# Block-sparse attention and a gated convolution FFN: a new written-out order, with six more dummy products on TensorE in the head

## The chip, the cores and the metric

The kernel runs on one core of a Trainium2 chip. Its engines work side by side, each through its own queue in order: TensorE (PE in the profile, with its weight loads as PEld), VectorE (DVE), ScalarE (ACT), GpSimd (POOL) and SyncE (SP). GpSimd, SyncE and ScalarE also issue DMA transfers. The metric is the device time of one execution, in microseconds (us). The median of the three runs shown here is the time that a kernel is judged by; one further execution was profiled.

## The reference

The inputs are q, k and v of shape 4 batches x 8 heads x 768 tokens x 64, in float32, and an integer table of sampled blocks. In short:

```python
scores = q @ k.T / 8                        # per batch and head, 768 x 768
mask   = |blk_i - blk_j| <= 1, first and last block rows and columns, 3 sampled blocks per row
attn   = softmax(where(mask, scores, -1e9))
x      = (attn @ v) as [4, 768, 512]        # heads side by side
h      = relu(x @ w_in)                     # 512 -> 1024
c      = conv_w[0]*h[s-1] + conv_w[1]*h[s] + conv_w[2]*h[s+1]   # along the tokens, per channel
out    = (h * sigmoid(c)) @ w_out           # 1024 -> 512, float32
```

## The kernel before, in words

**Attention.** All scores are computed, also masked ones: the mask is in 24 more rows (one per block of 32 tokens) that are appended to the 64 rows of q and k, so that one product over 88 rows gives score plus mask. The scores come out transposed (keys on the partitions). Two heads make a pair P, with 16 pairs in all; a query half of 384 tokens of one batch is a segment (the last one is cut in two, so there are 9). The scores of a segment are cut into units of 8 blocks of 128 x 128, and there are 144 units. A unit u is: two score operations `s` (number 2u and 2u+1, 512 columns of products each, line 761) into one of two PSUM tiles `st`; one `exp` on ScalarE over 128 x 1024 (line 773) into one of six tiles `pt`; two `av` operations of four 65-column products each (line 798). Score tiles alternate, so scores of unit u+2 wait until the exp of unit u has read its tile.

**FFN.** When a segment's four pairs are through, VectorE divides by the row sums (`rcp`, `norm`, line 709), the result is transposed (`x_tr` on TensorE with an eviction `x_cp`, or `x_xb` by a transposing DMA from SyncE), and TensorE multiplies with w_in (`f1`, line 895). The result goes through `relu` (ScalarE, line 915, or VectorE, line 917), the convolution is `mul` and `add` on VectorE (lines 947 and 955), then `tanh` on ScalarE (994), `g1` and `g2` on VectorE (997, 1002), the product with w_out (`f2`, line 830), an eviction `ev` (ScalarE or VectorE) and the store `out` from SyncE.

**PSUM.** Two score tiles of two banks, two banks `av`, two banks `mix`. The banks `mix` are shared by the transposes of q, k and x, by f1 and by f2, so each such operation waits for the eviction two users before it.

**Head.** Pair 0 is loaded in float32 over SyncE and ScalarE (`ld_k0`, `ld_q0`), cast (`cast_k`, `cast_q`), transposed (`k_tr`, `q_tr`, lines 460 and 500) and copied (`k_cp`, `q_cp`) beside the mask rows (`m_k`, `m_q`). All later pairs come over GpSimd's queue with a cast in the DMA (line 239). Before and between these, TensorE runs dummy products on a zeroed tile (line 230): 13 of 256 columns (`warm`) and NFILL of 128 columns (`fill`).

**Order.** Every operation is put into a graph by `op(name, ...)`, with the engines that may do it. Nothing schedules at run time: `put_down` reads the string `ORDER`, in which two letters name an operation by its place in the graph, one more letter names the engine where there is a choice, and one more the buffer where one is taken. So ORDER alone sets each engine's sequence, the split of evictions between ScalarE and VectorE, and which buffer each operation gets. In this document an operation is named by its name and its number in the graph, counted from 0 within the name (relu 2 is the third relu).

Of the kernel before, what the change touches and what calls it, by code (L numbers as in the profile page):

```python
# [21 lines left out]
0k0l1B00m0n0o0p1N11O1I01Z01/21AA202b1171CV1DV11G1vA0XV520535715810V5401G012V1HV1b0q0r0s0t0u0v0w0x0y5c00z5911P1
0A5d0K1S02d32e1V12725h11MA0135e25i5501QV11UV1TV1RV565a5b1J05m05n5j32r04M2p2140B5f0C5v15w5o45g5k5x51LV1KV1+V10L
1e11f5A05B2102415C05F15G0D0E5K05L5l5p5H15M25q15y22V225V26V23V5T15U5V35r02cV25z5D5s155Y05Z5E2f15+4611625I5J2i0
6352gV3660676802hV2kV2jV5N5O5W06b16c5X1W15/6d16k06l60646p16m26q65695P15Q6r3161i1XV2qV36a6e6g26h1h6u06v6f16n6o
6z16A6s6t6w46i06I06J1YV1j1k1d5t16x6y6B56N16C6O5uV06jV6K06D6P15R16S06T6U26L06M6E26F5SV6G00+6HV6X16Q1o6Y2s4N2l34O
2D04P1p1m2F14Q1c1n2G4R1q4S2EV42R16Z31lih1ii70071ie0ifigV0ijA7917a724ik1il2807e07f7b5iC0iEiD29V2aViFimA7g06R7j1
7k7l1in16VioipV6W7o07p2t06+iG7x17y6/iw173ix7q27z34T1r4U2T24ViK1iL2uV47502vViM767C07DiyA7417c7d7H17E47I2w17h7i
2m02xV2oV2yV7m7M07n7r7s7A07B7J52nV7N7t1iN77178V12SV07F7R17Siq0iriH7O07T17uiIisViJ0iO7+07/7G7K7L831848028537v1
2H07P7wV2IV07Q8807UiP7W22JViQ7V1898d181827X8a42U4W1s8e86it1iuivV4X1t4Y2+2iR8f58m08n7Y0878b7ZV8r18s8o08c2K18g8t1  # L30
iS2iT2MV8w08x8hiz08y28B18C8i02LV8jiAiBViV8p0iU8G08H8q8u8v8k18D3i+3j0iWi/8I48O18P8Q5j608T08U8V0322iX8z8A8E8F8J
8Y18K18R8S8Z2W02V12X8lV2ZVj12YV8+1910j792932j2jc1jd9919a8W8X8/90j39e09f944Z3034+31iYiZ2/V1959b3j8je9g59j19kj4
8L1j50/331349628M8N2jfjgV09l136V39j9jaA19o09p9q4jl13a03c9t1jmji0jnA35V9u971gjjjkV9B03e04/370509Cjr1js9c09d9v0
2z0512N1jG0jHjI3b3i9G19H2A09hjJ2CV2BVjK9D29L09i9MjtA9I39m9N5jo1jpjqV9Q1jx09Rjy9n9r9sjLjzA9S19Y09wju1jvjwA9Z3l
3m13o38V29x19EjO1jMjPjQjR9y0jW29+4a119F9Ja2jX9zjA0a60a7a30a823j13n3u3x3y2jSjT9K9O9P2O12PVjN2QVjZjYab19Tac9U9/0
jBjCV9V1983fjU9Wag0j+jb3q13d33p4ad3jD1aha0ai5jEjFAao1apa4a59Ak23ks0a9k3jV9Xk4k5k6aq1j/aaaeafat0auajak1ay1arav4
kg1asazkhaA0aD0awktaEaxk7aL1aMaBaCk0k1aF2kiku3raN3aQ0aRk8k9aGkjaS1aHkvkkA2al2am3hV3AaV1aWa+0a/3v2kwA3aX5b00aI0
aJ3gV3sV3C0ky1kz3kV3kAV1kB0kCkDVkW0kXkZaO0b31aPb4b52kN1aTbb0kH0aU3z3G3H03J3K33M3L3R3S1kIkOkJAkPAbcbg1bhbd4kY3tV
k+kE0kFkGVl21l3l4l5l6aYaZb1b2b6bl0kK1b71bebmbi3bfbq1kLbrkMVb81an0km0knbjla2lck/bn1by0lb3wV43B0ldbzl0b9kokpbs5l7
bA0kqA1bD1kT1bEkUbI0bJkQ0bF2kVAbK4l8leaKkxkl3N1kRkSVli3lkl11lfbN1l9ljlgllbkbobpbtbubv2lmka1bObP3bS0bT3Dlhbw3EV  # L40
3FVbU1kbkckdbB0keA3b+1b/c05bCbGbHlw0bLc30c4lxc81lnbMbQc9lq1lrc50ba3Ololpbxcd0ce3U3V03Z3Wkf3XjhlybRlzbVbW1ca2cf4
3PV13QVlAV2c1cl1cmcq0c2lscrcn3lC0lDcv13IV03TV1bX0bYcwcs1ltcx5lEVlF0lGlBlHVl+0l/m0m1m2cA0cBc6c7cblI0cF1cccGluA3
cC046471lJcgchlL1co0cH2lMcN0cpctcOlKAlNVci1m61m7cjcucS1cTm3cylO0lR1cP3cU13+0bZ1cX0cYczlPcDcElScZ5lQAm8m9cIcJ1m4
mamb3Y43lTVme2mgmfcK2mccLmhm5d01d1d80cQcRcVcWc+d9lU0lVd24da0dd1lWVdec/lX1df24b4849ck4c13/di0djd3lYdn1domdmidk3
d4cMdb04k4l2lZAdcmA0ds0dtmu14424adgdp1mm3momnmpd50mqdhd6du4mjmkml4pdA1dBmBdld7dC0mr40V242msdF0dGdmdqmvdrdvdw1
dK1dLdDdEdH2mCmwdIdP0dQdM3dR1mtmDmEV0lvdX1dYdx1dymxdJdNdOdSe00dTdZ44m4h4dmyA24ykre1e51e20e6e75mS0mV1mWd+0mTdz2
41VdU2dVea0ebef1mUV0mXAne0nfngnhni4q0dW4z3d/ege34n4i04D4Am/1e4ec3mY0en0eon0n1V4oeh1e8es1ete9edmZ4eV3m+V4fVnm1nn
45V2ep4njnknpnoeeeiek0elnqnl0mF4E1mzex0eymG1mHmImJez0eu5n20eC0mKA3eDej1eqereK1n3eE3em4rn4AeLeM4nrevn51n6eP0eweA
n7VeQeBeFeGeN0nb0eU1eVnu2eH1eInweR5eW0n81ncn9naAeZ0e+f21eOf3e/3nvnxmM1mNeSeTeXeYfa0f44ndVnsny4jV3nznC3fbf0f1nt
f5ff1f61fgfc5fh0mOeJmPnDnEfdfk0o00flnFfefp1o1mQA1o31fqo4nGnH4sV4nAnB4tVo2Afm3nInJo5AnQ0nR4B4v4w14CmRmL4Ffx0fy  # L50
4xV4oq0osfr2nSnK1fz4fC1fDnTfH04J4K2fIfE14LV0orotounUV0fJ5ovnLnMnNfM1fNnOA2f724GV0f84HVfifR0fjnW0nXnZ1n+fnfO0nYA
n/AfS4ufofsftfZ1f+o90owoxfA0oaoi1okfT3ojfu0olfvomg20fBg3fFo61o7f/2g44obAg71fGfKfLg8fPfQo8Voy2fUozfW1onnVf904g4I
fwof0gc0g91oBoooAopgdge5oc1odoeAgk1ogohAglfV1g0g1g5gp0gm0oU1gqg6gaoVgu1gbgvgfggoO0oPoCoG3oHoJoIfXoKgr3oDgw2gn0
gD0gogsgtgEgI1gJoLgh2oEoFgigF4fYgK1oWgxoQgN0gOoMoNoXoYV1gP5gygW1oRgXp41p5p6g/0p7gjoSA3h0gY0gz0p8A0pa0pbpd1peh41
pcV1pfVpy0gAh13pAh5hd0pj0pg1pkphgG1h62nPoZplApiAhegHgLhi1gMgQgRhf4pzpBgB0gCA1gZ0g+hjpp1pG1pCpHpIpJpKhn0hk1pDpq
pm0pnpoAprAgS1gThohw1pO2pPpEpRhxhy5h2h3h7h8ps0pto+1o/hg1p0hhpuAp1h92pQpLhp0pMpF1pShahB1gU0hChlhmhqhrp2A2gVAhs0
hthD3pv1pwhb0hz0hK0pxAhcVpThLhM2pNhu0hvVhAhT1hUqh1hEqipW3pYqn0hY0hG1qoqjApXpZp+hV4hF1hNhOq21p/hZi51i6qpApUhHpV
q0hP2q3hW0hI0q4q1h+1q5hJV2hXqe0qfhQqy0qAqzi70qBh/i01i8i9q6A1qk1qgAi10i2i30qlqO1qq2ia1qrqPibi4AqmAp9p3qtqsqG3q80
q9hR1hSAqaic1idAqbqcA0rf1rgrhAr60r7quqvqCqIqRqwq7qdoTqxr8AqDrx0rc1rdryreAri1rjr90raqEqFrz2rk0r01rAqHrBqJrlrmqK
qQrs0rtr1rbArn1ru2qW0rorp0rqrrqLqXrC0rI1rO2rJrPrvqSrwqMqTqUqNrDrQrKrRrLrMA2rSArNqVr2rTr3r4V1r5qYqZq+A0q/rErF  # L60
# [989 lines left out]
```

## Time and profile before

| what | value |
|---|---|
| median of three runs | 207.91 us (207.61 to 208.0) |
| the profiled execution's own time | 207.34 us |
| its span, first to last instruction | 205.5 us |
| TensorE busy | 198.0 us (96%) |
| VectorE busy | 185.2 us (90%) |
| ScalarE busy | 190.7 us (93%) |
| GpSimd busy | 60.8 us (30%) |
| moved by DMA | 25.20 MB |
| exp of one unit (line 773) | 144 of 1044 ns on average |

The span lies 1.84 us below the execution's own time; those 1.84 us lie around the instructions. The busy time of an engine can overlap itself, since its instructions are pipelined: an exp that the profile shows with 1.02 to 1.08 us is followed by the next 0.90 to 0.92 us after its start. Waits are read from the idle time before an instruction and from what is named behind the arrow as its releaser. In the chain of waits, a piece belongs to the engine that was waited for.

### The profile page before, as it was taken

The numbers are of one execution on the slowest core, as the hardware profiler recorded it, in microseconds if no ns is written. First come the engines' busy times: TensorE is split into PE (matmuls) and PEld (weight loads), VectorE is DVE, ScalarE is ACT, GpSimd is POOL, SyncE is SP. The second block draws the span as 40 slices with busy tenths as digits, with TensorE's granted clock in tenths as the row PEclk, the third lists the DMA queues.
The fourth block names the chain that finished last, engine by engine and source line by source line (L and its number), as shares of the span: only waits on it lengthen the run. The fifth ranks groups of instructions, "written<-read, shape, count | busy, mean of one in ns | idle before, by whom it ended". The sixth has DMA issues, their size and how long they took to land.

```text
span 205.5 us, 6234 instructions
## 1 busy us (share of the span) xinstructions
PE 198.0 (96%) x2395; PEld 142.9 (70%) x2415; DVE 185.2 (90%) x575; ACT 190.7 (93%) x252; POOL 60.8 (30%) x114
## 2 busy tenths in 40 slices
PE   7999999999999999999999999999999999999991
PEld 5678877877667766666677767677577757786750
DVE  5999999999999999999979977999999929999970
ACT  6999999999999999999899999999999988998842
POOL 8897555302733243202343248500000000000000
PEclk9999999999999999999999999999999999999998
DMA  6999999991889998994979399996521131011205
GB/s 138 206 193 188 186 148 148 153 180 27 107 107 150 153 182 131 134 170 66 196 96 121 71 120 175 172 200 116 148 82 26 23 126 46 3 51 56 102 9 198
DMA packets 49305, 25.20 MB, mean 123 GB/s; under 512 B 35100, under 2 KB 46332, under 8 KB 49276
## 3 DMA queue, kind: packets, MB, share of 16 engines
...
q1 hardware_dynamic: 29260, 13.46, 30.9%
...
## 4 chain that ended last, share of the span: by engine, by line
PE 72%; ACT 18%; DVE 4%; issue 3%; DMA 2%; ACTq 0%
PE st L761 22%; PE mix L830 17%; PE mix L895 17%; ACT pt L773 15%; PE av L798 12%; DMA o2s<-in_k_dram 2%; DVE m L947 1%; PE st L830 1%; DVE t L331 1%; ACT t L327 1%; PE av L966 1%; ACT nat L327 1%; PE mix L728 1%; ACT o2s L327 1%; ACT m L994 0%
## 5 line engine op out<-in xcount | busy, mean ns | idle before, releaser
L773 ACT ACTIVATE pt<-st 128x1024 bf16<-128x1024 f32 x144 | 141.0, 1044 | 2.6 <-PE st L761 1.6
L761 PE MATMUL st<-t 88*128 88x256 bf16 (+2 forms) x600 | 91.7, 267 | 0.9 <-ACT t L327 0.2
L798 PEld LDWEIGHTS <-pt 128*128 128x128 bf16 x1152 | 53.7, 97 | 13.1 <-ACT pt L773 0.4
L761 PEld LDWEIGHTS <-t 88*128 88x128 bf16 x600 | 48.8, 97 | 19.9 <-issue 1.2
L798 PE MATMUL av<-vt,pt 128*128 128x65 bf16 x1152 | 60.0, 193 | 0.1
L895 PE MATMUL mix<-xT,winb 128*128 128x384 bf16 (+2 forms) x288 | 54.7, 307 | 0.3
L947 DVE TENSOR_SCALAR m<-hE,cw 128x382 bf16<-128x382 bf16 (+2 forms) x192 | 48.5, 313 | 0.3
L830 PE MATMUL mix<-woutb,gT 128*128 128x512 bf16 x157 | 44.4, 379 | 0.6
L955 DVE TENSOR_TENSOR m<-m 128x764 bf16<-128x764 bf16 (+2 forms) x64 | 34.1, 534 | 0.6
L895 PEld LDWEIGHTS <-winb 128*128 128x128 bf16 x288 | 24.1, 97 | 9.0 <-issue 1.0
L994 ACT ACTIVATE m<-m 128x764 bf16<-128x764 bf16 (+2 forms) x32 | 26.7, 835 | 0.6 <-DVE m L955 0.6
L830 PEld LDWEIGHTS <-gT 128*128 128x128 bf16 x200 | 17.3, 97 | 10.2 <-DVE gT L1002 0.6
L407 POOL COPY pace<-pt 1x1 bf16<-1x1 bf16 x24 | 7.7, 322 | 53.4 <-ACT pt L773 53.4
L917 DVE TENSOR_SCALAR hE<-mix 128x384 bf16<-128x384 f32 x26 | 14.5, 556 | 5.7 <-PE mix L895 5.3
L915 ACT ACTIVATE hE<-mix 128x384 bf16<-128x384 f32 (+2 forms) x38 | 18.4, 501 | 0.9 <-PE mix L895 0.5
L1002 DVE TENSOR_TENSOR gT<-m,hE 128x764 bf16<-128x764 bf16 (+3 forms) x36 | 18.2, 511 | 0.6
L709 DVE TENSOR_TENSOR xtok<-av,rcp 128x384 bf16<-128x384 f32 (+2 forms) x36 | 18.3, 507 | 0.5
L239 POOL DMA_DIRECT2D nat<-in_q_dram x23 | 17.1, 743 | 2.3 <-issue 1.0
L331 DVE COPY t<-mix 64x384 bf16<-64x384 bf16 (+1 forms) x33 | 13.3, 411 | 0.8 <-PE mix L460 0.3
L997 DVE TENSOR_SCALAR m<-m 128x764 bf16<-128x764 bf16 (+3 forms) x36 | 12.1, 337 | 0.5 <-ACT m L994 0.3
L239 POOL DMA_DIRECT2D nat<-in_k_dram x15 | 11.4, 762 | 2.7 <-issue 2.1
L331 DVE COPY t<-stg 64x1536 bf16<-64x1536 bf16 x20 | 11.5, 578 | 0.3
...
## 6 DMA issues: line engine op xcount, KB each, us to landing
...
```

Of the source, the lines that this page charges most:

```text
L239: return op(name, {eng: occ}, lambda e: on(e).dma_start(out=dst(), in_=src), prio, deps, dma=(kind, service), **kw)
L331: nc.vector.tensor_copy(out=dst, in_=src)
L709: nm = op("norm", {"DVE": t_dps(128 * C)}, lambda e: nc.vector.tensor_tensor(out=xtok_t[xk.index][:, 0:C].rearrange("p c h d -> p h c d"), ...
L761: nc.tensor.matmul(out=st[:, 128 * x:128 * (x + n_)], lhsT=t[0:88, 12 + 6 * hh + kc, :], rhs=t[0:88, idx:idx + (n_ - 1) * (2 if P < NPE el ...
L773: nc.scalar.activation(out=pt_t[ptb.index][:, c0:c1], in_=st_t[stb.index][:, c0:c1], func=AF.Exp, bias=0.0, scale=0.125)
L798: nc.tensor.matmul(out=o[:, off:off + 65], lhsT=pt_t[ptb.index][:, 128 * x:128 * x + 128], rhs=V_t[vslot_b[P].index][:, hh, kc, 0:65], sta ...
L830: nc.tensor.matmul(out=acc(), lhsT=gT_t[gb.index][:, ffc, 128 * t:128 * t + 128], rhs=woutb[:, ffc, c0:c1], start=(ffc == 0), stop=(ffc == ...
L895: nc.tensor.matmul(out=mix_t[hb.index][:, w1 * y:w1 * y + w1], lhsT=winb[:, fc, 128 * ffc:128 * ffc + 128], rhs=xT_t[xt_buf[n].index][:, f ...
L915: nc.scalar.activation(out=dst, in_=src, func=AF.Relu, bias=0.0, scale=0.5)
L947: nc.vector.tensor_scalar(out=m_t[cb.index][:, x, y, 0:w], in0=hE_t[heb.index][:, f0 + y, t0 + x:t0 + x + w], scalar1=cw[:, x, f0 + y:f0 + ...
L955: nc.vector.tensor_tensor(out=m[:, a_, :, 0:w], in0=m[:, a_, :, 0:w], in1=m[:, b_, :, 0:w], op=ALU.add)
L994: th = [op("tanh", {"ACT": t_act(2 * w) + 0.04}, lambda e, cb=cb, w=w: nc.scalar.activation(out=m_t[cb.index][:, 0, :, 0:w], in_=m_t[cb.in ...
```

## The change

NFILL goes from 26 to 32, so that six more dummy products of 128 columns are in the graph, and ORDER is replaced by another one. Since six operations are inserted early in the graph, all codes behind them shift; the letters can't be compared directly. Decoded, the same operations are there, each with the same instructions. The whole diff, with the ORDER strings cut to their first and last lines:

```diff
 ORDER = """
-0G0002119030405060F18011a0708090a0b0c0d0e0H0f0g0h0i0I0J0M0N0R0O0Q0P0ZA1uV00S0T1wA0YA1xA1y01E11zV01FA0WV0VA0U0j
...
-rGA3rH
+000210M030405061f010708090L0O0N0S0U0T1T00W0V13V1e0a1h0X12A1AV11CA1U1O02302520Y1g1d0Z0b262h10c0d0e0f0g0h0i0j0k
...
+r4A0r5
 """
...
     SW = 0.715
-    NWARM, NFILL = 13, 26
+    NWARM, NFILL = 13, 32
     SPLIT = ()
```

What the new order moves, by engine:

- TensorE: 13 fills before the first scores instead of 11 (6, then 7 behind the transposes of pair 0, where there had been 4, 3 and 4); 12 instead of 9 between the scores of units 1 and 2; 7 instead of 6 later. The transposes k_tr 0, q_tr 0 and k_tr 1 follow each other without fills between them. q_tr 2 stands behind the scores of unit 4 instead of ahead of them. s 98 stands ahead of f1 18 instead of behind it. k_tr 5 stands behind the scores s 56 and s 57 instead of ahead of s 54, and q_tr 8 takes its bank.
- 23 operations change between ScalarE and VectorE. To VectorE: m_k 1, cast_q 1, relu 2, 23, 26, 33 and 38, ev 3, 11 and 24, x_cp 13. To ScalarE: k_cp 3, q_cp 10, relu 16, 20, 22, 32, 35, 39 and 48, ev 7, 13 and 21.
- ScalarE: exp 54 stands ahead of relu 12 and 13 instead of behind them; tanh 0 ahead of exp 29.
- VectorE: the band of the mask (a1) is computed ahead of ident24; relu 2, mul 5 and v_cp 5 stand ahead of k_cp 11; v_cp 7 ahead of ev 1; norm 12 ahead of g2 7.
- GpSimd: ld_q 5 two places later; ld_v 2 ahead of a pace; ld_k 4 ahead of ld_win 1; ld_k 7 behind ld_v 6 and ld_nq 0. Pair 0's tile nat and that of pair 1 change places.
- SyncE: m_turn 1 behind xb 3, xb 4 ahead of x_xb 0, x_xb 3 behind xb 7, and several stores at other places.

More of the change, by code (lines that the diff above doesn't have):

```diff
@@ L20 @@
 ORDER = """
-0G0002119030405060F18011a0708090a0b0c0d0e0H0f0g0h0i0I0J0M0N0R0O0Q0P0ZA1uV00S0T1wA0YA1xA1y01E11zV01FA0WV0VA0U0j
[L22 to L60, printed above, removed]
@@ L61 @@
-rGA3rH
+000210M030405061f010708090L0O0N0S0U0T1T00W0V13V1e0a1h0X12A1AV11CA1U1O02302520Y1g1d0Z0b262h10c0d0e0f0g0h0i0j0k
+1E01FV01K11DA1H01LA0P0l0m0n0o0p0q0r10V0/A1GA1IV0+17G1BV1JA11V580595d15e16V2j31M01/118V2d21NV0s0t0u0v0w0Q0x0y0z
+0A0B0C0D5a05f12k1SA05i01V15j5k20E1Y00F5n15o5b0191WV11ZV1+V5c5g1XV0G0H5s05t5p32x10I0R0J1P05u41a5B15C5D524V15h1k1
+5l5m1RV1l1QV5G05H2712a05I05L15M5N15q0K5r5v5Q05R28V22cV5S25w15E5F5J2bV29V5Z15+5/35x05y1b2iV25K5O620632l06442mV3
+2nV671686955P2o12pV2qV5T6c06d5U6005z06h16i6e06165666a6q06r6j12v26s26b6f6g6v16w5V11c5W5X15AV01o5YV2wV31j6x36A06B
@@ new lines @@
+6k6m26l16t6F16G2006u6y6C46z6O06P6D4S2y1u4T2r34U2J06E1n1p21V6H522V6n1q6Q06I6T16U6J6o16K06L6R06Y06Z6S6pV6M06V16NV
+6+21i711726W7331r1s2KV41tin1io76077ik0ilimV0ipAiI07847f17g6X6/2e12gV7k07liq07h5iKiJ4V2L01v4W2M4X1w4Y2X14Z1x4+
+2Z22fAirisViL7p17q70it1iu7m07u07vivViQ1iRiM4/2+501y511z527r17w2743425375797a17D17E7F3iC0iDiEA7I07J2z17i7j7n2C0
+7o7s7K47t7x7N17O7b1iS2YV0iN7P52AV42BV2DV2EV2s17y7S07Tiw0ix2tV2uV7ciOiT7z2iU7X17Y7G07d17H7U0840857L7M7Q7R7Z114
+3008918a7V7W7+8627eV17AiyV8b37B17/187882N08e08f8j18kiP08007CViz1iAiV8g48c8d8s08t8l5812OV02PV8h2Q08iiBViY28u08x1
@@ new lines @@
+8y8miF18C08D363543755iG8n8z12RViZ2SVi+8E22/131iW8H18I3918208v08w8J38M08N8A8B8FiHVi/8o183V8O48G8U18V8W5jc18p8Z0
+8+8/0iXj43j53a8K8L8P92193jd8q09708Q18X988Y909419132Vj0j78rVj6ji0jjj133V3d0562F03829f19gj8992j23f3g13i3h3o35V195
+969aj3j99k09b9l9h3jajkje8R29p19qjb3eV29c0158S9m4jljmV0jf9r5jgA19u09v9z19w03bV3cVjr0jsjo1jtA572T19Ajp9B13p13r3k0
+9H09I9J29d1m8T29ejx0jy9i09jjzA3l9M19N9n9o9R02G09S9O39T4jqVjM0jNjOjP2HV3s23w1jQ2IVju19sjvjR9W19X9t9x9y9CjD0a20
+9D13u3tjwVjU1jVjW9E1jXa3jA1jBjE9K9Y5a409FjYjSa71a8ac09L9PjCAjFAa91adae29Q2U19U9V9Z9+a50a6ah1aaabjJ0k022WVk12VV
@@ new lines @@
+k3jTk2aiam0jG1anjZaj3ao59Gj+k4j/3x9/23v4jHjKau1afjLAavjIVagakaz0aw0aAaB1k5km0kn3D3E0ky1aE1aFaJ0aKkzk83k9alapka
+kba0aG2kckdaL3k6k7ar0keasaq1axayaC3A3B2aDaHaR1aSaIkAkoaT4aW0aXaMaNkfkBaY0kpa/1b0b40b5aO13qV3aPkqV23GkCA3a13j3
+3yVb15aU0aVkE1kH0kIkFb91bab62aZ3zVkGA13F3Pa+bb3b2kN1kObh0bibm1bnb3kPAkJVl00l1l2kK0bj4bo0b7kT1kLb8br0bs3M3Q33S
+3N03R3XkUbcbw13CV4l3l43nVl5kMVl81bxks0kVAl93mVlabt1lbbe2by5jnbd1bkkQ1lcblkRkSAbE0bFktbG2lg2lilhbJ1bKbL3ljlkat0
+3I1kDjh3J3T03Y1bpkukvkwA0bfbqkZ1k+ldaQbgk/Vl6l71bO0bPbQ4kW0kXbukYAkxbvlo3lplqlllmlebzbAbT1bH0bIbUbB03H03U3LVbY0
@@ new lines @@
+bZb+0bV1kg1bMkhkibNkjc40bClrlnlskkA3c5c91cabRbSbWbXb/c65cb2lC0ltlw1c01ce0cfcj1ckcg3lfcl43KVc11lulvlDlElxlFlGA1
+cr0bDcscw1cxc7c8lI0ct1lJ3OV0cy53VV1c2lKV3ZV13WVlycB0cClL0lM3+3/1434041cG1cHcccdcD0cI2lNVm40m5m6m7lzlO0chcL0cicm
+cMlAA0cnlPcT1cUlR1lScu0cvco2m8cN3lQVcpm9cY0czcAcZcEcFcJcKcOcV1d11d2c+5cP1lU0d30d60d7lTVmc1mdmemfcQ0lX1lVlYd83mg
+cRmac31lZVde1dfcWdj0cXc/d0lWAmbmk2mll+0mhdg54c4d2dkd4d5d9l/da424h494edo1dpmimnmmm0Vdl2lHm11m2dq4dh0m3A441klcScq
+dt0du4a2mjdv1momG0mpdy1mHdidmdzdnms3lBdG0mtmu45db1drdsdHmvdcmwdA3mA1dwdxmBdBmqdL1dMdC1dI5dQ0dJdKmr4qmxdRdN2mImC
@@ new lines @@
+mymzdddV1dO4f4r0dS4dWmJe104g4n4o0e2dX1e35dD0mKV146V2dPdTdUmDe61dYdZe7eb0ecmY0mZmEA34v4s4i0e80m/1ed3dEd+24E4F34J
+eg1n0d/m+A047V4bV2n1Vnk0nmnlnnehe40e5e9el0emdF24jei44w14tn50n21ean6et1euen1n7Aev5n3ey0eeezefejn80eD1ekeEeA0eF3
+mFn4Vnons1ntnv4kV3n9mM1eoeI0ep1eJewexeBeC4pV3eQ1naAeK4kr48eq1nuernwnpeReS5nxnb0mNnc4lVndVeGeHeLmOmPeMmQA0mLeV0
+4GeWe+1e/ne0eX0nh1eT0niese0nA2nCeN0eOnBnqnr0nDnEePeUf30f03f4njAnff81f9ngV4u4B4C14DV4nI3nJf52fa4mS1mTfg0fheYnynz
+mUfl1eZfmf1f2fi5nFmVo60nKfn04xfq0f6o7f7frfbfv1fc1fjfwfkfoo8AmWV3nL4yV4o91oafs34zVnGnM4m4K04H4ImX4Lfx2fpftnHfD0
@@ new lines @@
+fEfI1obAfJnQ0nRow0nNnOoxoznPoyfd1oAfF4nW1nXfN0fOfK5nYfP0funZnSnTfS1fTfyfz4MV04P4Q2n+A2o31o4oBnUA14NVoCfA2oDfU1
+o00fB4RV0o1o5Ao2AfX0fYg31fefG1of1g4fZ3ogoc0g80fHfLg9odoo1opg52ohAga4oroqosotgd1fMfQfRoeVoE2oFfVgefWf+gf5ouoHgi0
+gjgk0g00oGovf/0g6g7gboi1ol0omojonAgq1grgv0okAgcgs1g1oIoM3oNoJoOoPoKo+0ggghglgwgmgt1gx3gA1gBoU1oVff0nV4AfCn/4Ogu
+o/gJ0gKgC2gygzgO1oQgn1oLgPgDgEgooRgL4gQ5p0oWgT0gUoSoToXoYA3p1p2V1h01h1pa1pbgV0h21pcpdh50h6ha1peA2gF2gGh73g2gpmR
+pg0phpfpj1pkpiA1plVpE0pFpHhbpGhc2pm0pnpoAgM0pp1pqprAhj0hkgNgRhl4pM1pOgSpv0pNpIpPpwpxAho1gH1gIA1hpht0hugWhq5ps0
@@ new lines @@
+ptgXh31h4gY0pQpuAhC1p41p5p6h8h9hDhdpJpU2gZpVpXpWhepKhf1pYhv0pRg+0g/Ap7hm0hE1hnhrpy0pzp8A0pAApShghH0hshIhwhxhh1
+hQ1pL1hiVhy2hzhJ3pB0pChRpDAhS2hA1pThBVhF1hGhZ0h+hKq03qn0qopZq1q2hM0q3qpAhL0hTi21i3qt1p+q4quhNqE0q80h/4hUp/q5hV1
+q6q7ib0q9qvAqGqaichO1i01i1qbi45i5hPV2id0qcA2qU1hWi72qFi8qk1qlqmAi60ieifqVqHig0qw2ihqq0qyqIi91qriaAqsAqe1qfhX0qJ
+qghYVii0qhp9ijAqxqKqzrl0rmqAqM3qNqiA0rnAqBrc1rdrD1ri0rErjreAqCqLqDrkAro0rprq0rF2rf1rgr60p3oZqdqjqOry0r7rrrGqPrs
+qWqQqXrHrhArt1rurv0qRr01r1rzrwqSrxrA2rU0rBrCqYqZrI1rO2rPqTq+q/rVrJrWrQrRrXrSA1rYVrKrTrZrLrMA3rNr8r9raA2rbr2r3
```

## The prediction

> **What bounds the kernel now.** I read the page's shares first, then the busy time by stretches, the timelines of the head and the chain of waits. The page:
>
> ```profile
> PE 198.0 (96%) x2395; PEld 142.9 (70%) x2415; DVE 185.2 (90%) x575; ACT 190.7 (93%) x252; POOL 60.8 (30%) x114
> PE 72%; ACT 18%; DVE 4%; issue 3%; DMA 2%; ACTq 0%
> ```
>
> The stretches give start:end, length, then the busy time of PE, PEld, DVE, ACT and POOL, the granted clock, the DMA share and GB/s:
>
> ```profile
> 18.00:40.00 22.00, 21.88 (x328) 17.43 (x326) 21.26 (x77) 21.80 (x27) 11.71 (x26) 1.00 1.13 165
> 40.00:60.00 20.00, 19.75 (x253) 14.38 (x252) 19.40 (x56) 19.89 (x25) 6.75 (x14) 1.00 0.73 106
> 60.00:80.00 20.00, 19.82 (x257) 14.20 (x257) 19.62 (x60) 19.95 (x26) 7.16 (x13) 1.00 1.12 145
> 80.00:103.00 23.00, 22.78 (x248) 15.38 (x251) 22.31 (x61) 21.62 (x28) 4.87 (x9) 1.00 0.90 150
> 103.00:200.00 97.00, 96.26 (x1136) 68.71 (x1145) 87.08 (x277) 90.38 (x129) 15.00 (x27) 1.00 0.55 91
> ```
>
> From 18 to 80 us TensorE, VectorE and ScalarE are all full; from 103 us on TensorE alone is (VectorE 90%, ScalarE 93%). So the time is TensorE's work, plus the stops into which VectorE or ScalarE drives it. Behind 24 us the trace shows some twenty stops, together 2.2 us: the most that better order could win there. The head, TensorE and then ScalarE:
>
> ```profile
> 1.06 3.38 PE L230 MATMUL av<-warm 128*128 128x256 bf16 x17 [1.06 <-DVE warm L223]
> 5.85 0.39 PE L230 MATMUL av<-warm 128*128 128x128 bf16 x4
> 6.47 1.06 PE L761 MATMUL st<-t 88*128 88x384 bf16 x8 [0.23 <-ACT t L327]
> 11.03 0.33 PE L522 MATMUL mix<-ident,nq 128*128 128x128 bf16 x3 [0.29 <-DVE t L331]
> ...
> 5.11 0.51 ACT L327 CAST nat<-o2s 128x384 bf16<-128x384 f32 x1
> 5.53 0.47 ACT L327 COPY t<-mix 64x384 bf16<-64x384 bf16 x1
> 6.02 0.40 ACT L327 COPY t<-mtok 24x256 bf16<-24x256 bf16 x1
> 6.95 0.35 ACT L327 CAST nat<-o2s 128x192 bf16<-128x192 f32 x1
> 7.32 1.02 ACT L773 ACTIVATE pt<-st 128x1024 bf16<-128x1024 f32 x1
> ```
>
> Pieces of the chain of waits (start, length, engine, tile and line, count) that the steps below come back to:
>
> ```profile
> 30.06 1.63 DVE m L947 x6
> 34.76 0.46 DVE t L331
> 37.91 0.33 PE mix L728 x3
> 56.48 0.69 DVE o2s L331
> 57.22 0.48 PE mix L895 x2
> 65.42 1.04 ACT pt L773
> 66.51 0.60 PE st L761 x4
> ```
>
> The scores wait for q_cp 0 (5.53) and m_q (6.02) on ScalarE, not for TensorE. At 37.91 x_tr 4 has waited .21 us for q_cp 17, at 57.22 f1 18 has waited .30 for ev 1 (both VectorE), at 66.51 s 112 .24 for exp 54 (ScalarE).
>
> **The change part by part.** Costs per instruction, start to next start, from the rows: exp .91, mul .46, relu .47 on VectorE and .37 on ScalarE, k_cp .47, q_cp .28, v_cp .27, ev .61 and .47, g2 .47. Products of 128 columns follow each other at .107 before 5.5 us and at .056 from 5.68.
>
> *Fills.* Six more cost 6 x .056 = .34 us. Two stand ahead of the first scores, where TensorE stops .40 for ScalarE; three between units 1 and 2, and one later. There exp (.91 a unit) sets the pace against .45 of scores. Taken 0; if the cover were gone, .34. Below nothing only through the clock, rival D.
>
> *Start.* m_k 1 (.70 on ScalarE, some .42 on VectorE) goes into VectorE's .59 us idle before 4.03, so cast_k 1 starts at 4.39 instead of 5.11. But q_cp 0 can't use that: k_tr 0 now stands behind 6 fills (4.45), q_tr 0 ends at 5.41, q_cp 0 starts at 5.45, m_q runs 5.94 to 6.34, and the first scores start at 6.39 (-.08). Some .3 us of TensorE's stop stay. k_cp 3 (.50) replaces cast_q 1 (.37) ahead of the first exp: exp 0 at 7.37 (+.04).
>
> *q_tr 2* (waiting until 11.03) no longer stands ahead of s 8: exp 4 at 11.74 (-.09). exp 7, whose transposes now wait for cw (13.46) and q_cp 2 (13.8), comes at 14.66 (-.09). VectorE: k_cp 6 starts about .2 later, k_cp 8 stands at 17.85 as before. From 30.06 to 37.87 the chain is VectorE's, so ScalarE's .09 is lost there. Head together 0; bounds -.09 (all kept) and +.15 (cast_q 1 late on VectorE).
>
> *relu 2, mul 5, v_cp 5 ahead of k_cp 11.* VectorE has .47 + .46 + .27 more and q_cp 10's .28 less ahead of it: +.92, about 36.9 us. k_tr 5 was moved back, and the next user of its bank, q_tr 8, arrives at about 36.7: TensorE waits .2, and x_tr 4's old .21 shrinks, as q_cp 17 has .28 less ahead. Net +.07; bounds -.21 (stop gone) and +.5.
>
> *relu 2, v_cp 7 ahead of ev 1.* +.47 + .27 - .28 = +.46 for f1 18. s 98 moved ahead of it covers .22. +.24; bounds -.30 (its present stop) and +.46.
>
> *exp 54 ahead of relu 12 and 13.* The two (.74) had held the exp that s 112 waited for. -.24; if relu 13 is then late for its product, 0.
>
> *norm 12 ahead of g2 7.* With its rcp and a moved eviction it puts .76 more VectorE work ahead of g2 7, whose products f2 22 and 23 started .06 and .5 us behind it in before. +.2; bounds 0 and +.5.
>
> *The other evictions.* Summed over the run, VectorE loses .84 us of work and ScalarE gains .5; ahead of relu 24 VectorE has 1.5 less: the .10 stop before f1 50 goes. -.10; bounds -.3 (small ones go too) and +.2 (ScalarE, 93% busy).
>
> *Tail.* Its last outputs keep their order and f1 120's .31 wait for ev 19 stays. x_cp 13 on VectorE puts g2 28 later: +.07; bounds 0 and +.15.
>
> *GpSimd and SyncE.* ld_q 5 goes out about 10.5 instead of 8.99 and lands 5.8 later, read by the transposes of segment 1: 0. Behind the paces, loads run ahead: 0. m_turn 1, behind xb 3, is issued at 45.7 instead of 38.6 and first read by s 99 at 58.4: 0, cover 12 us. The stores are read by nobody. Bounds together 0 and +.2, should a late transposing DMA hold f1.
>
> Sum: 0 + .07 + .24 - .24 + .2 - .10 + .07 = +.24. The profiled execution's own time is 207.34 (span 205.5 + 1.84 around it), so 207.6 for such a one; it stands .57 below the median of the runs, 207.91, so 208.1 by the median.
>
> **The rivals.**
>
> *A, faster.* The new order does what the old failed at: f1 18's .30, s 112's .24, x_tr 4's .21 and f1 50's .10 go, and nothing comes in their place, as VectorE carries .84 us less in all. -.85; the products of g2 7 and the tail give .3 back: 207.91 - .55 = 207.4. For it: TensorE's work is the same, and every stop is under .35 us, so small shifts decide. Against: VectorE is full just where relu 2 is put on it.
>
> *B, slower: VectorE's queue.* Between 30 and 60 us VectorE idles nowhere more than .2 us, so the +.92 ahead of k_cp 11 is passed on. From a lag of .5 us there, TensorE meets it three times: x_tr 4 and q_tr 8 (+.4), f1 18 (+.46), the products of g2 7 (+.5), less .34 for s 112 and f1 50: +1.0, 208.9. For it: the 30.06 to 37.87 chain. Against: relu 2 and q_cp 10 were exchanged, so ScalarE's queue gets lighter there, and TensorE has av products to do first.
>
> *D, slower: the clock.* Before, fills separated the transposes; now nine transposes (k_tr 0, q_tr 0, k_tr 1) follow each other, up to 1.3 us of no other product just where the step falls from .107 to .056. If that reading had to begin anew and took its 4.6 us (1.06 to 5.68) again, 45 products of scores, transposes and fills up to the exp of unit 2 cost .05 more each, 2.3 us, of which TensorE's spare time takes about 1.1: +1.2, 209.3. Against: in before the rise came with six transposes among the last twelve products.
>
> The Trainium skill (TensorE: Matmul & The Clock Gate, Part 4: PE-mode transpose) says that transposes do not count as busy for the clock, and in Part 1 that the clock rises after a busy window of about 3.4 us which runs freely. By that rule an estimate is a rise one window later, near 9 us, and a time as under D; the trace's rise 4.6 us after the first product allows it, and its column of granted clock, 1.00 throughout, shows nothing of it.
>
> **How the numbers follow.** The runs shown span .39 us, so about 0.2% (.42 us) is what a measurement can tell from no change. The forecast, 208.1, has .38 (own range 207.8 to 208.6: same .28, slower .07, faster .03). A has .30 (faster .27, same .03), B .25 (slower .24, same .01), D .07 (slower). Together faster .30, same .32, slower .38. The range reaches into A to 207.1 (.06 left below) and through B to 209.0 (.14 left above with D).
>
> **What would show it.** First scores at 6.4, exp 0 at 7.37, exp 4 at 11.74, exp 7 at 14.66; the step falling to .056 between 5.5 and 5.8 us (at 9 if D holds); q_tr 8 waiting for k_cp 11 at 36.9; f1 18 waiting .3 to .5 for VectorE; no stop before s 112. With A the stops behind 24 us sum to 1.6 or less instead of 2.2, with B to 3 or more. I am wrong if the order of the evictions moves stops to places that I did not follow: after 103 us I looked at the engines' loads and the tail, not at each pair of neighbours.

## The result, and the profile after

The changed kernel takes 210.25 us (median of 4 runs, 209.97 to 210.51) against 207.89 us: a ratio of 1.0115, with a 95% interval of 1.0098 to 1.0133. It is 2.4 us slower. The forecast was 208.1 with a range up to 209.0. The profiled execution took 209.97 us with a span of 208.2 us, 2.7 us more than before's 205.5. (The kernel before and those made from it lie about 2 us above their usual time in a part of their executions, which widens their intervals and lifts some medians below.)

The changed kernel's page, its shares and the chain by engine:

```profile
PE 199.0 (96%) x2400; PEld 144.0 (69%) x2421; DVE 185.1 (89%) x574; ACT 192.5 (92%) x253; POOL 61.1 (29%) x114
PE 54%; DVE 27%; ACT 12%; issue 4%; DVEq 0%; ACTq 0%
```

Its busy time by stretches (columns as in the prediction):

```profile
18.00:40.00 22.00, 21.52 (x310) 16.79 (x309) 21.04 (x75) 21.63 (x26) 10.65 (x23) 1.00 1.18 168
40.00:60.00 20.00, 19.77 (x259) 14.41 (x259) 19.62 (x57) 19.69 (x24) 6.95 (x16) 1.00 0.88 119
60.00:80.00 20.00, 19.62 (x256) 14.32 (x257) 19.24 (x60) 19.66 (x26) 6.98 (x12) 1.00 0.81 121
80.00:103.00 23.00, 22.84 (x249) 15.40 (x251) 20.80 (x60) 22.99 (x30) 5.84 (x11) 1.00 1.09 138
103.00:200.00 97.00, 95.50 (x1128) 68.48 (x1140) 87.62 (x277) 90.73 (x128) 14.59 (x27) 1.00 0.56 95
```

The work is the same, but TensorE is idle .36 us more between 18 and 40 us (21.88 busy before) and .76 us more between 103 and 200 us (96.26 before), and VectorE's share of the chain that ends last went from 4% to 27%. The starts of the exps, changed kernel minus before, tell where the time came in (the two orders place an exp differently among its neighbours, so a single value in the middle is good to some .3 us; exps 13 to 20 all stand near .64, 92 to 101 near .91, 124 to 130 near .96):

| exp | 12 | 13 | 40 | 48 | 56 | 62 | 90 | 128 | f1 120 | end |
|---|---|---|---|---|---|---|---|---|---|---|
| later by, us | .21 | .64 | .62 | .85 | .70 | 1.06 | .89 | .96 | 1.93 | 2.7 |

So .64 came in the head, about .3 in all between exp 13 and exp 128, and 1.74 behind that, in the last 23 us. The head, on TensorE, ScalarE and VectorE and with GpSimd's copy:

```profile
6.42 1.10 PE L761 MATMUL st<-t 88*128 88x384 bf16 x8
8.03 0.36 PE L500 MATMUL av<-ident,nat 128*64 128x128 bf16 x3 [0.51 <-DVE nat L331]
20.36 0.38 PE L761 MATMUL st<-t 88*128 88x384 bf16 x2 [0.20 <-DVE t L331]
...
5.47 0.47 ACT L327 COPY t<-mix 64x384 bf16<-64x384 bf16 x1 [0.73 <-PE mix L500]
7.27 1.94 ACT L773 ACTIVATE pt<-st 128x1024 bf16<-128x1024 f32 x2
...
6.56 0.61 DVE L299 SCALAR_TENSOR_TENSOR mtok<-sbi,keyid,A 24x384 bf16<-24x384 int32 x1
7.20 0.77 DVE L331 CAST nat<-o2s 128x192 bf16<-128x192 f32 x1
18.44 1.11 DVE L331 COPY t<-mix 64x768 bf16<-64x768 bf16 x2
...
6.87 0.99 POOL L329 COPY t<-t 24x768 bf16<-24x768 bf16 x1
```

Beside it, the cast of cast_q 0 and the start of k_cp 8 on VectorE in before:

```profile
4.03 0.26 DVE L331 CAST nat<-o2s 128x192 bf16<-128x192 f32 x1 [0.59 <-DMA o2s<-in_q_dram]
17.84 1.78 DVE L331 COPY t<-mix 64x768 bf16<-64x768 bf16 x4 [0.31 <-PE mix L460]
```

The first scores and exp 0 stand where they were forecast. But cast_q 1, now on VectorE, takes .77 us; the same cast on ScalarE had taken .35, and cast_q 0 on VectorE .26 in before. q_tr 1 waits .51 us for it, VectorE is .60 us later at k_cp 8 (18.44 instead of 17.84), and at 20.36 s 27 waits for q_cp 13 on VectorE.

The tail, again by engine (ScalarE, TensorE, VectorE):

```profile
184.97 0.84 ACT L994 ACTIVATE m<-m 128x764 bf16<-128x764 bf16 x1
186.91 0.60 ACT L915 ACTIVATE hE<-mix 128x512 bf16<-128x512 f32 x1 [1.10 <-DVE gT L1002]
...
187.56 0.22 PE L728 MATMUL mix<-ident,xtok 128*128 128x128 bf16 x1 [0.64 <-ACT hE L915]
201.47 1.02 PE L830 MATMUL st<-woutb,gT 128*128 128x512 bf16 x4 [0.61 <-DVE o2s L331]
...
201.00 0.42 DVE L331 COPY o2s<-st 128x256 f32<-128x256 f32 x1
```

In before, the same two places (tanh 27 and relu 59 on ScalarE, then x_tr 12, and the last products on TensorE):

```profile
184.04 0.84 ACT L994 ACTIVATE m<-m 128x764 bf16<-128x764 bf16 x1
184.77 0.60 ACT L915 ACTIVATE hE<-mix 128x512 bf16<-128x512 f32 x1
...
185.52 0.22 PE L728 MATMUL mix<-ident,xtok 128*128 128x128 bf16 x1
198.78 1.90 PE L830 MATMUL mix<-woutb,gT 128*128 128x512 bf16 x8
200.51 0.81 PE L830 MATMUL st<-woutb,gT 128*128 128x512 bf16 x3
```

In the changed kernel ScalarE stands idle 1.10 us ahead of relu 59 until g2 27 (line 1002) is done, and x_tr 12 waits for relu 59; in before relu 59 did not wait for g2 27. At 201.47 f2 90 waits for ev 24, the eviction of another output. In before f2 90 waited for an eviction of the other bank of its tile as well, ev 23, but that was done by 199.7 us, and f2 90 stood behind eight products that lasted beyond 200 us. The new order puts f2 90 and 91 ahead of those eight.

### The profile page after: what moved, and what is told of

The parts are those of the page before. It is cut to its first block, busy times and chain, and to the rows that moved or that the text cites. A ratio compares the mean times of both kernels' runs of the same rounds, so it can differ in the third digit from the quotient of the medians.

```text
span 208.2 us, 6227 instructions
## 1 busy us (share of the span) xinstructions
PE 199.0 (96%) x2400; PEld 144.0 (69%) x2421; DVE 185.1 (89%) x574; ACT 192.5 (92%) x253; POOL 61.1 (29%) x114
## 4 chain that ended last, share of the span: by engine, by line
PE 54%; DVE 27%; ACT 12%; issue 4%; DVEq 0%; ACTq 0%
PE st L761 17%; PE mix L830 12%; PE mix L895 12%; PE av L798 10%; ACT pt L773 9%; DVE m L947 7%; DVE t L331 5%; DVE m L955 4%; DVE gT L1002 2%; DVE xtok L709 2%; DVE m L997 1%; DVE hE L917 1%; ACT m L994 1%; ACT o2s L327 1%; PE mix L728 1%
## 5 line engine op out<-in xcount | busy, mean ns | idle before, releaser
L761 PE MATMUL st<-t 88*128 88x256 bf16 (+2 forms) x600 | 89.3, 268 | 0.6 <-DVE t L331 0.2
L798 PEld LDWEIGHTS <-pt 128*128 128x128 bf16 x1152 | 52.8, 97 | 13.1 <-issue 1.3
L798 PE MATMUL av<-vt,pt 128*128 128x65 bf16 x1152 | 59.3, 193 | 0.6 <-DVE xtok L709 0.2
L895 PE MATMUL mix<-xT,winb 128*128 128x384 bf16 (+2 forms) x288 | 53.7, 308 | 0.2
L947 DVE TENSOR_SCALAR m<-hE,cw 128x382 bf16<-128x382 bf16 (+2 forms) x192 | 49.7, 319 | 0.6 <-ACT hE L915 0.3
L830 PE MATMUL mix<-woutb,gT 128*128 128x512 bf16 x155 | 42.3, 379 | 0.7
L915 ACT ACTIVATE hE<-mix 128x384 bf16<-128x384 f32 (+2 forms) x40 | 20.0, 512 | 1.8 <-DVE gT L1002 1.1
L917 DVE TENSOR_SCALAR hE<-mix 128x384 bf16<-128x384 f32 x24 | 13.3, 554 | 5.2 <-PE mix L895 4.7
L239 POOL DMA_DIRECT2D nat<-in_k_dram x15 | 11.9, 795 | 1.7 <-issue 1.4
```

Source lines behind the costliest of these rows:

```text
L239: return op(name, {eng: occ}, lambda e: on(e).dma_start(out=dst(), in_=src), prio, deps, dma=(kind, service), **kw)
L761: nc.tensor.matmul(out=st[:, 128 * x:128 * (x + n_)], lhsT=t[0:88, 12 + 6 * hh + kc, :], rhs=t[0:88, idx:idx + (n_ - 1) * (2 if P < NPE el ...
L798: nc.tensor.matmul(out=o[:, off:off + 65], lhsT=pt_t[ptb.index][:, 128 * x:128 * x + 128], rhs=V_t[vslot_b[P].index][:, hh, kc, 0:65], sta ...
L830: nc.tensor.matmul(out=acc(), lhsT=gT_t[gb.index][:, ffc, 128 * t:128 * t + 128], rhs=woutb[:, ffc, c0:c1], start=(ffc == 0), stop=(ffc == ...
L895: nc.tensor.matmul(out=mix_t[hb.index][:, w1 * y:w1 * y + w1], lhsT=winb[:, fc, 128 * ffc:128 * ffc + 128], rhs=xT_t[xt_buf[n].index][:, f ...
L947: nc.vector.tensor_scalar(out=m_t[cb.index][:, x, y, 0:w], in0=hE_t[heb.index][:, f0 + y, t0 + x:t0 + x + w], scalar1=cw[:, x, f0 + y:f0 + ...
```

## The experiments

Times are medians beside runs of the kernel before on the same chip. Edits are given with decoded names, in the order in which the operations are put down.

**1. Is relu 59's wait made by the order in ORDER, or by the tail's load?** relu 59 writes columns 385 to 640 of rows 6 and 7 of the tile hE; g2 27 reads columns 1 to 382 of the same rows. No data passes between the two, and the graph has no edge between them. In before relu 59 is put down first, in the changed kernel g2 27. The two programs as built show it:

```text
changed kernel:           relu 59 waits for VectorE, TensorE, ScalarE
relu 59 put down first:   relu 59 waits for TensorE, ScalarE
```

```diff
-g1 27, g2 27, s 286, f2 73, relu 59
+g1 27, relu 59, g2 27, s 286, f2 73
```

> The changed kernel with one edit: relu 59 is put down ahead of g2 27 instead of behind it. Each engine's sequence stays the same; only what waits for what changes. Theory (order sets the wait): relu 59 waits 1.10 us for g2 27 because both touch the same rows of the tile hE and g2 27 was put down first. Then relu 59 starts near 185.7 instead of 186.91, the .81 stop before x_tr 12 and the .18 behind it go: -.8 to -1.0, about 209.4. Rival (the tail has too much VectorE and ScalarE work): relu 59 starts earlier, but the next instruction waits instead, and the time moves by less than .3.

Measured: 209.22 us, 1.0 below the changed kernel. Every engine's sequence is as it was. ScalarE and TensorE in this run:

```profile
185.56 0.84 ACT L994 ACTIVATE m<-m 128x764 bf16<-128x764 bf16 x1
186.29 0.61 ACT L915 ACTIVATE hE<-mix 128x512 bf16<-128x512 f32 x1
...
187.35 0.22 PE L728 MATMUL mix<-ident,xtok 128*128 128x128 bf16 x1
```

relu 59 follows tanh 27 without idle time, and x_tr 12 without a stop (this execution's head was .6 us later, so the clock times don't compare). The reverse, in the kernel before:

```diff
-relu 59, g1 26, norm 32, g2 26, g1 27, rcp 33, f2 73, ..., g2 27
+g1 26, norm 32, g2 26, g1 27, rcp 33, g2 27, relu 59, f2 73, ...
```

> The kernel before with g2 27 put down ahead of relu 59, every engine's sequence unchanged (the same edit as planted once before). Theory: relu 59 waits for g2 27 until about 186, as in the changed kernel, x_tr 12 comes about 1 us later: +.7 to +1.0, 208.6 to 208.9. Rival: the wait is filled by other work of TensorE, under +.3.

Measured: 208.88 us against 207.88 (ratio 1.0061, 1.0031 to 1.0090), with the same wait on ScalarE and TensorE (the four executions of a first run of the same edit lie from 212.45 to 229.54 us, too far apart to be used):

```profile
186.35 0.60 ACT L915 ACTIVATE hE<-mix 128x512 bf16<-128x512 f32 x1 [1.10 <-DVE gT L1002]
...
187.01 0.22 PE L728 MATMUL mix<-ident,xtok 128*128 128x128 bf16 x1 [0.96 <-ACT hE L915]
```

So the wait is made by which of these two operations on one tile is put down first, and costs 1.0 us here, taken away or put in.

**2. f2 90 and ev 24.** f2 96 to 99 write the first bank of score tile 0, which ev 24 reads; f2 88 to 91 write its second bank.

```diff
-f2 96: score tile 0, first bank
+f2 96: score tile 1, second bank
```

> The changed kernel with one edit: the products f2 96 to 99 go to the second bank of the other score tile, so that ev 24, which reads them, no longer shares a tile with f2 90. Theory (order and tile set the wait): f2 90 waits for ev 24 although it writes another bank of that tile; with the other tile f2 90 starts at 200.7 instead of 201.47, f2 91 then waits for g2 31 until 201.1, and the end comes .7 to .8 earlier: about 209.5. Rival (g2 31 is simply late): f2 90 or 91 still waits and less than .2 is gained.

Measured: 209.33 us, .9 below the changed kernel. TensorE now runs through (21 and 8 products, no idle time between):

```profile
198.75 3.22 PE L830 MATMUL st<-woutb,gT 128*128 128x512 bf16 x21
201.80 1.89 PE L830 MATMUL mix<-woutb,gT 128*128 128x512 bf16 x8
```

So a product into one bank of a tile waited for the eviction of its other bank. In before f2 96 was in score tile 1, and the users of tile 0 stood in another order.

**3. cast_q 1 and GpSimd's copy.**

```diff
-VectorE: k_cp 2, a5 1, cast_q 1, m_q 1
+VectorE: k_cp 2, cast_q 1, a5 1, m_q 1
```

> The changed kernel with one edit: on VectorE, cast_q 1 stands ahead of a5 1 instead of behind it. Theory (GpSimd's copy and this cast slow each other): cast_q 1 took .78 because it ran beside the copy on GpSimd (6.87 to 7.86); starting at 6.56 it takes .26 to .45, q_tr 1 stands at 7.5 to 7.6 instead of 8.03, VectorE reaches k_cp 8 some .3 to .5 earlier than 18.44, and the .37 stop before s 27 shrinks: -.3 to -.6, 209.65 to 209.95. Rival (the cast takes .78 on VectorE anyway): q_tr 1 comes .6 earlier all the same, but VectorE is as late at k_cp 8 as before, and no more than .2 is gained.

Measured: 210.2 us: nothing gained, so the theory's gain failed. In this execution the cast began at 7.02, inside the copy, and took .52. The next run shows why the place of the cast alone can't help.

> The changed kernel with the three edits together. If the three causes are separate places, their gains add: -.9 - .75 - .3 to .6, so 208.0 to 208.3, within .4 of the kernel before (207.89). Rival (the tail's loads are the limit, or a later start only fills the gap): the sum falls short by half, 209.2.

Measured: 208.3 us, 1.95 below the changed kernel: the two tail edits add up, the third adds nothing. VectorE and GpSimd in this run:

```profile
6.57 0.34 DVE L331 CAST nat<-o2s 128x192 bf16<-128x192 f32 x1
6.94 1.16 DVE L299 SCALAR_TENSOR_TENSOR mtok<-sbi,keyid,A 24x384 bf16<-24x384 int32 x1
...
6.88 0.82 POOL L329 COPY t<-t 24x768 bf16<-24x768 bf16 x1
```

The cast, ahead of the copy, takes .34; now a5 1 stands beside the copy and takes 1.16 instead of .60. To test this by itself, the kernel before with the same three instructions of VectorE exchanged:

```diff
-VectorE: m_q 0, a5 1, k_cp 2, k_cp 3, m_q 1
+VectorE: m_q 0, k_cp 2, k_cp 3, a5 1, m_q 1
```

> The kernel before with one edit: on VectorE, a5 1 stands behind k_cp 2 and k_cp 3 instead of ahead of them, so that it runs beside GpSimd's copy m_h1 1 (6.76 to 7.58) and the two evictions from PSUM don't. Theory (beside that copy, VectorE's instructions that read SBUF alone take about twice as long, those that read PSUM don't): a5 1 takes 1.1 to 1.2 us instead of .60, VectorE is .5 to .6 later at m_q 1, and since its idle before k_cp 8 is .31, the time grows by .2 to .6: 208.1 to 208.5. Rival (the lengths of cast_q 1 and a5 1 had other causes): a5 1 takes .60, nothing changes.

Measured: 210.71 us by the median of twelve executions, four from 208.16 to 209.01 and eight from 210.37 to 212.82; the ratio of 1.0057 (1.0006 to 1.0109) mixes the two groups, so the size rests on the trace, whose execution took 208.39, as expected. In before a5 1 ran ahead of the copy, and the two evictions from PSUM beside it. Before, then this run:

```profile
6.05 0.60 DVE L299 SCALAR_TENSOR_TENSOR mtok<-sbi,keyid,A 24x384 bf16<-24x384 int32 x1
6.70 0.33 DVE L331 COPY t<-av 64x384 bf16<-64x384 bf16 x1
7.05 0.36 DVE L331 COPY t<-av 64x384 bf16<-64x384 bf16 x1
6.76 0.82 POOL L329 COPY t<-t 24x768 bf16<-24x768 bf16 x1
```

```profile
6.09 0.35 DVE L331 COPY t<-av 64x384 bf16<-64x384 bf16 x1
...
6.84 1.12 DVE L299 SCALAR_TENSOR_TENSOR mtok<-sbi,keyid,A 24x384 bf16<-24x384 int32 x1
6.73 0.82 POOL L329 COPY t<-t 24x768 bf16<-24x768 bf16 x1
```

a5 1 grows by .52; VectorE is .56 us later at m_q 1, .71 at k_cp 8, and the span grows by 1.0 us, by an exchange of three instructions with equal work. Not all of the 1.0 need be the exchange's: .3 of it came in between exp 28 and exp 32, where the trace of s 98 alone (experiment 6), which has no edit in the head, lost as much.

**4. Undoing the head.** With both tail edits, first the exchange of engines alone, then also a5 1 ahead of k_cp 2.

```diff
-ScalarE: k_cp 1, k_cp 3, exp 0        VectorE: k_cp 2, a5 1, cast_q 1, m_q 1
+ScalarE: k_cp 1, cast_q 1, exp 0      VectorE: k_cp 2, a5 1, k_cp 3, m_q 1       (exchange alone)
+ScalarE: k_cp 1, cast_q 1, exp 0      VectorE: a5 1, k_cp 2, k_cp 3, m_q 1       (head undone)
```

> The changed kernel with both tail edits and, of the head, only the exchange undone: cast_q 1 on ScalarE, k_cp 3 on VectorE; a5 1 stays behind k_cp 2. Theory (the cast on VectorE beside GpSimd's copy is the lag): a5 1 starts before the copy and keeps .6, k_cp 3 takes the cast's place with .35 instead of .77, VectorE is at k_cp 8 at 17.9 to 18.1, and the time is that of the run with the head undone (207.9) within .2. Rival (a5 1's place matters too): it lies half way, 208.1 or above.

> The changed kernel with both tail edits (relu 59 ahead of g2 27, the other bank for f2 96) and the middle of its head as in before: cast_q 1 on ScalarE, k_cp 3 on VectorE, and a5 1 ahead of k_cp 2 and 3, so that GpSimd's copy runs beside evictions from PSUM. Theory (VectorE's .6 us at k_cp 8 come from cast_q 1 and the copy on GpSimd): VectorE reaches k_cp 8 at 17.8 to 18.0, the .37 stop before s 27 goes, exp 13 stands at 20.2 instead of 20.8, and the time is .4 to .6 below the run with all three edits (208.3): 207.7 to 207.9. Rival (the lag comes from the other moves of the head, k_tr 3 and q_tr 5 behind cw): VectorE is still late by over .4, 208.2.

Measured: 208.01 us for the exchange alone, 207.88 for the head undone (ratio to before .9984, .9952 to 1.0016). VectorE reaches k_cp 8 at 18.14 and 18.02. The exchange is most of what counts, and with the tail edits it brings the changed kernel back to the time of the kernel before; that it beats it isn't shown. By the medians undoing the head is worth .3 to .4 us (from 208.3), less than the .64 of the changed kernel's trace, and the executions of the three overlap. Together the parts make up the slowdown: 1.03 for relu 59, .92 for f2 96 and .42 for the head are 2.37.

**5. The fills.** The kernel with the head undone, less fills 11, 12, 22, 23, 24 and 30.

> The run before this one (tail edits and head undone) without six dummy products: two ahead of the first scores, three between units 1 and 2, one before q_tr 2. Theory (they lie in TensorE's waits): first scores, exp 2 and exp 4 at the same times within .05, and the same time within .2. Rival (they cost .34, or they hold the clock up): -.3, or a step of .107 that lasts longer and +.2 or more.

Measured: 208.03 us, .15 more, within the scatter. In its profiled execution exp 4 came .43 us later, not within the .05 expected, because v_cp 0 waited for the load of v:

```profile
9.68 0.83 ACT L327 CAST vt<-m 128x768 bf16<-128x768 f32 x1 [0.52 <-DMA m<-in_v_dram]
```

**6. Terms of the middle.** norm 11 ahead of mul 21, in the kernel with the head undone:

```diff
-relu 14, mul 21, mul 22, mul 23, add 14, norm 11
+relu 14, norm 11, mul 21, mul 22, mul 23, add 14
```

> The changed kernel with both tail edits, the head undone and norm 11 ahead of mul 21 instead of behind add 14. Theory (norm 11, not norm 12 and g2 7, is what TensorE lost at 75 us): the .38 stop before av 117 goes, and .2 to .4 of it stays gained: 207.5 to 207.7. Rival (VectorE is full there, so mul 21 to 23 and g2 6 and 7 come .47 later and TensorE meets them): the same time, 207.9, with the stop before f2 22 grown by as much.

Measured: 208.05 us, no gain, as the rival had it: the stop before av 117 is gone, one of nearly as much has come before f2 22, which waits for g2 6:

```profile
76.59 1.04 PE L830 MATMUL mix<-woutb,gT 128*128 128x512 bf16 x4 [0.19 <-DVE gT L1002]
```

Then the two moves that should have helped, in the kernel before:

```diff
-exp 53, relu 12, exp 54                  f1 18, s 98, f1 19
+exp 53, exp 54, relu 12                  s 98, f1 18, f1 19
```

> The kernel before with the two moves of the change that should have helped: exp 54 ahead of relu 12, and s 98 ahead of f1 18. Theory (a stop of TensorE that goes is time gained): the .24 before s 112 and .22 of the .30 before f1 18 go: 207.4 to 207.6. Rival (VectorE or ScalarE takes it back within the next 20 us, as their work there is unchanged): 207.8 to 207.9.

Measured: 211.95 us, 4 us slower (ratio 1.0201, 1.0150 to 1.0253). VectorE, then TensorE in this run:

```profile
67.03 1.16 DVE L947 TENSOR_SCALAR m<-hE,cw 128x386 bf16<-128x386 bf16 x4 [0.77 <-ACT hE L915]
...
70.28 0.48 PE L895 MATMUL mix<-xT,winb 128*128 128x384 bf16 x2 [0.72 <-DVE t L331]
82.99 0.97 PE L895 MATMUL mix<-xT,winb 128*128 128x384 bf16 x5 [1.73 <-DMA xT<-xtok]
```

relu 12 ends at 67.00 instead of 65.55, mul 18 on VectorE waits .77 for it, and f1 30 waits .72 for q_cp 23 behind that. The longer stop, 1.73 us, is that of f1 33, for a transposing DMA of SyncE, and it has another source: pace 3, a one-element copy with which GpSimd holds back its next load until an exp has written its tile `pt`. GpSimd in this run, then in before:

```profile
66.74 0.18 POOL L407 COPY pace<-pt 1x1 bf16<-1x1 bf16 x1 [10.91 <-ACT pt L773]
67.20 0.70 POOL L239 DMA_DIRECT2D nat<-in_k_dram  x1 [0.28 <-issue]
```

```profile
58.45 0.24 POOL L407 COPY pace<-pt 1x1 bf16<-1x1 bf16 x1 [2.95 <-ACT pt L773]
58.90 0.70 POOL L239 DMA_DIRECT2D nat<-in_k_dram  x1 [0.21 <-PE st L761]
```

pace 3 reads one element of the tile that exp 48 has written and that exp 54 writes next. In before it is put down ahead of exp 54 and waits for exp 48. This edit puts exp 54 down ahead of it, and pace 3 waits for exp 54 and runs 8.3 us later. ld_k 8 goes out behind it, SyncE's next transposing DMA, which waits for that load, is issued at 70.73 instead of 64.44, and f1 33 waits for one of those behind it. So it is the same kind of wait as in experiment 1, made by the edit unintended. By the exps' starts, .3 of this trace's 3.9 us stands there before either move, some 1.3 came with relu 12, and 2.2 at f1 33; no run takes pace 3 back by itself.

To separate the two moves, s 98 alone in the kernel before, and relu 12 alone taken back in the kernel with the head undone:

> The kernel before with s 98 ahead of f1 18 and nothing else. Theory (the 4 us lost by the run with two moves came from relu 12, put behind exp 54, for which VectorE's mul 18 and 19 waited; s 98 only covers f1 18's wait for ev 1): f1 18's .30 stop shrinks by .2, and the time is that of the kernel before or up to .2 less, 207.7 to 207.9. Rival (s 98 took part in the loss): over 208.3.

> The changed kernel with both tail edits and the head undone (207.88), and relu 12 ahead of exp 54 again, as in before; relu 13 stays behind. Theory (the prediction's term): exp 54 and with it s 112 come .37 later than now, TensorE stops .2 to .4 before s 112, and the time grows by .2 to .4: 208.1 to 208.3. Rival (VectorE sets the pace there, as it did in the kernel before, and mul 18 can start no sooner or later): TensorE's stop comes and is given back within 10 us, 207.9.

Measured, s 98 alone: 209.01 us by the median of twelve executions (ratio 1.0040, 1.0007 to 1.0073), with five from 207.66 to 208.35. By that number the rival holds. The trace is of one of the five, at 207.83, and shows no gain and no loss where s 98 stands: f1 18's .30 stop is gone, s 99 has one of .19 instead, for stg_cp 2 on VectorE, and exp 44 and exp 62 both stand .4 later than in before, most of which came in between exp 28 and exp 32, ahead of s 98. Why the other executions took longer stays open. relu 12 back: 208.65 us, .77 more, with this stop before s 112:

```profile
67.25 0.38 PE L761 MATMUL st<-t 88*128 88x256 bf16 x2 [0.61 <-ACT pt L773]
```

exp 54 ahead of relu 12 is worth .8 us in the changed order. In the old one the same move, with s 98's, cost 4 us, but more than half of that stands at f1 33, behind pace 3, so the price of a late relu 12 alone isn't shown there.

## Why the prediction was wrong

Forecast against the changed kernel's trace; the measured column goes by the profiled execution's exps, so single steps of the middle are good to some .3 us.

| step | forecast | measured |
|---|---|---|
| first scores, exp 0 | 6.39, 7.37 | 6.42, 7.27 |
| exp 4, exp 7 | 11.74, 14.66 | 11.93, 14.97 |
| VectorE at k_cp 8 | 17.85 | 18.44 |
| head | 0 (-.09 to +.15) | +.64 |
| k_cp 11, q_tr 8, x_tr 4 | +.07 | -.02 |
| f1 18 | +.24 | +.23 |
| exp 54 | -.24 | -.15 |
| g2 7 | +.2 | +.36 |
| other evictions | -.10 | -.17, then +.07 |
| tail | +.07 (0 to +.15) | +.97 and +.77 |

*The step "Start" failed in cast_q 1.* I named "cast_q 1 late on VectorE" as an upper end and gave it .15, with the length of cast_q 0 in mind (.26), which had run beside no copy. Beside the copy it took .77, and the lag of VectorE, .60 us at k_cp 8, came through in full at s 27. In that execution the head lost .64; by the medians of experiment 4 it is .3 to .4. Experiment 3 shows that it isn't the cast as such: of two instructions of VectorE that read SBUF, the one that stands beside GpSimd's copy is held up, be it the cast or a5 1.

The Trainium skill (SBUF — State Buffer, SBUF: two separate sides) says that VectorE and GpSimd share one pair of SBUF ports as an exclusive lock: of a GpSimd instruction and a VectorE one in a two-port mode or with two SBUF inputs, the one that starts first holds the pair for its whole length, and the other is blocked. The traces agree in the main: a5 1 took .60 to .61 when it started first (in the changed kernel the copy then took .99), and 1.12 and 1.16 when the copy had started .06 to .11 us before it, while evictions from PSUM kept .33 to .36. A block for the whole of the copy would have made a5 1 about 1.31 in experiment 3's exchange and the changed kernel's cast about 1.0, where 1.12 and .77 were measured, so a full block isn't shown.

*The step "Tail" failed, by 1.7 us.* "Its last outputs keep their order" was not so: the last stores are outputs 23, 24, 21, 20, 22 in before and 23, 24, 22, 21, 20 in the changed kernel, and with output 22 moved f2 90, ahead of the products that had covered its wait. And the order in which things were put down around them changed as well: that made relu 59's wait, 1.0 us, beside the .9 for f2 90. I read ORDER as each engine's sequence and looked for waits in the graph's edges and in the buffers. It also decides, for two operations on one tile, which waits for which. Both waits could have been seen before the run: relu 59 stands ahead of g2 27 in the old string and behind it in the new, and f2 96 moved into the tile of f2 88. The prediction's own sign of being wrong, stops at places that it did not follow behind 103 us, came true.

*The middle* was forecast at +.17, and the trace shows +.3; but the trace with the head undone shows .45 for the same stretch, while by the medians that kernel takes the time of before. So it lies somewhere between 0 and .45, which neither confirms the sum nor refutes it, and it was not right in every part. q_tr 8 starts .06 behind k_cp 11, but TensorE stands idle only .05 for it (forecast .2); av 54 waits .25 for norm 4 instead. Beside f1 18's .21 for ev 1 (forecast .3 to .5), f2 6 waits .20 for g2 2. exp 54 ahead of relu 12, taken as -.24, was worth .77 in experiment 6. At 75 us it is av 117 that waits, for norm 11 (.38 by the products' steps): norm 11 had moved from ahead of mul 21 to behind add 14, which neither the list of moves nor the prediction has. The prediction's products of g2 7 were a misreading: what started .06 and .5 behind its operand in before were f2 14 and f2 22, and the operand was g2 6.

*The fills* cost nothing, as forecast; *GpSimd's and SyncE's moves* showed no stop in the changed kernel's trace.

*The rivals.* A's gains are there in part, but VectorE takes them back: experiment 6 shows it for norm 11, and in the one trace of s 98 alone for f1 18. B's price was of the right kind for the head, a lag of VectorE that TensorE meets, but its place was wrong: the lag arose at 7 us, not at 37, and the tail's waits were of no rival's kind. D (whose 209.3 is counted from the forecast, where A and B count from before's median): the step of .107 lasted until the first scores at 6.42 instead of 5.68, later than the forecast's 5.5 to 5.8, at no cost, as only fills ran meanwhile. The order isn't its cause: in the exchange on VectorE in the kernel before (experiment 3), whose TensorE has before's sequence, the fall came between 6.1 and 6.6; in the exchange of engines alone (experiment 4), with the changed kernel's sequence, between 4.6 and 5.0.

The Trainium skill (TensorE: Matmul & The Clock Gate, Part 1) says that the window runs freely, so that the rise of the clock varies by some 500 ns either way. A rise that varies with the same sequence agrees with that, but the spread here is wider, from 4.1 to 6.6 us over sixteen traces, and the measurement decides. That transposes don't count as busy could not be told here.

What stays open: with both tail edits and the head undone the profiled span was 206.1 us, .6 above before's; .23 of it stands at exp 13 already, and the rest wasn't taken apart. A head without GpSimd's copy wasn't tried, nor the two tail edits without a third. Why operations on one tile wait for each other although their columns or banks differ isn't shown; shown is that the order decides it. It isn't so on every tile: in the run with the two moves of experiment 6, products that read other columns of the tile xT ran from 80.61 while f1 33 waited until 82.99 for the DMA into its last columns.
